# Operand addresses on multiples of 512 bytes, small tiles at the right edge, and centroid temporaries in the weight staging buffers

## The chip, the cores and the metric

The kernel runs on one core of a Trainium2 chip. The metric is the device time of one execution in microseconds; lower is better. A core has TensorE (PE; its weight loads are a row of their own, PEld), VectorE (DVE), ScalarE (ACT), GpSimd (POOL) and SyncE (SP), which here only issues DMAs. They work on SBUF, 128 partitions wide; an address below is a byte offset within a partition. PE writes to PSUM.

## The reference, cut to what matters

Three stages in float32. First an attention in which a key is seen by a query only if both are nearest to the same of 16 centroids of their head; then a mixer over tokens and channels; then a second one with a cosine and a sine.

```python
# attention, B=2, H=8, S=768, D=64, 16 centroids a head
q_assign = np.argmax(np.einsum('bhsd,hcd->bhsc', q_n, c_n), axis=-1)
k_assign = np.argmax(np.einsum('bhsd,hcd->bhsc', k_n, c_n), axis=-1)
mask = q_assign[:, :, :, None] == k_assign[:, :, None, :]
scores = np.where(mask, scale * np.matmul(q, k.transpose(0, 1, 3, 2)), -1000000000.0)
x = softmax(scores) @ v                       # then heads side by side: B x 768 x 512
# mixer 1
u = x + (np.maximum(xt @ w_tok1, 0.0) @ w_tok2).transpose(0, 2, 1)
x = u + np.maximum(u @ w_ch1, 0.0) @ w_ch2    # 512 -> 1536 -> 512
# mixer 2
theta = x @ w_theta
u = x + w_tok_r @ (x * np.cos(theta)) + w_tok_i @ (x * np.sin(theta))
out = u + np.maximum(u @ w_ch, 0.0)
```

The weights, q, k and v arrive as float32 or, for the weights, as float64 words.

## The kernel before, in words

**Products.** Each float32 operand is split into a high part (rounded to PE's one-pass float32 format, `F32R`) and a low part, the rest. A product then is three matmuls into one PSUM bank (`mm3`, L117 to L123): high by low, low by high, high by high. Every matmul has a stationary operand of 128 columns, which a weight load brings in, and a moving operand of 256, 384 or 512 columns that is streamed past it, four bytes a column and partition. Transposes (L408, L451, L562, L578, L702) are matmuls of 128 float32 columns against an identity matrix.

**Attention** (L156 to L510). Heads are taken in pairs. For a pair, `masks` (L240) multiplies queries and keys with the normalised centroids (tiles `csth`, `cstl`, stationary), transposes the similarities on DVE (tile `sT`), takes the maximum, compares, transposes back, keeps the first maximum with a triangular matrix (`pp`, L275) and leaves one-hot rows (`oh`, then `m`). They are appended to the query and key operands, so that `scores` (L381 to L388, out tile `s`, four matmuls of 384 columns) gives scores with the mask in them. A unit is two tiles of 128 queries of one head: `scores`, a row maximum on DVE (`nm`, L391), the exponential on ACT (`e`, L393), then `turn` (transposes `t` of `e`, and their split into `ph` and `pl`), then `values` (`o`, 12 matmuls of 256 columns). 48 units run in a software pipeline: unit n's scores, unit n-1's `turn`, unit n-2's `values`.

**The first pair.** Its masks need only the unsplit centroids `cst` (L250). `place_centroids` (L205 to L213) splits the centroids for the other pairs: a copy on ACT (`cth`), a subtraction on DVE (`ctl`), and then, after two memsets on POOL, four small casts on DVE that place them in `csth` and `cstl`. In the text it stands behind the first masks and the first heads' preparation (L469); the tile framework's scheduler, which orders each engine's instructions by its own simulation of the program, decides where they go.

**Mixers** (L524 to L734). Token mixing (`g`, `h`), then for channel mixing `r` (up, L617) and `c` (down, L625), then `th`, `y` and `po`, all with 512 columns (the last `po` in two halves). Each weight tile is loaded raw by DMA (512 KB into one of three buffers, tag `wraw`), converted on ACT, DVE and POOL, and split (`load_w`, L95).

**Where operands lie.** Tiles are carved out of pools one after the other, so small tiles shift what comes behind them. The program's allocation before, as the offset of each family of tiles modulo 512 bytes:

| tiles | role in products | offset mod 512 |
|---|---|---|
| `q2`, `k2`, `qh`, `k1` (`s`; q and k splits for `sim`) | both operands | 160 |
| `vs` | stationary of `o` | 160 |
| `e`, `ph`, `pl` | `ph`, `pl` moving of `o`; in token mixing moving of `g`, `h` | 416 |
| `uh/ul`, `rh/rl`, `zh/zl` (tag `blk`) | moving of `r` and `y`; stationary of `c`, `th` | 160 |
| weights' `h/l` parts (tag `wg`) | moving of `c`, `th`, `po`; stationary of `r`, `y` | 480 |
| `csth`, `cstl` | stationary of `sim` | 0 |
| `ident`, `xn` | transposes | 128 |

A slice of an operand starts a multiple of 512 bytes behind its tile's start, so these hold for slices too. The families at 480 lie in the upper part of SBUF (from byte 163808), those at 160 and 416 below byte 152000.

```python
halfpi = const.tile([P, 1], F32, name="halfpi")                       # L68
scratch = ap.tile([P, S], F32, tag="xt", bufs=2, name="scratch")      # L165
csth, cstl = (mp.tile([P, H // 2, 224], F32R, name=f"cst{k}") for k in "hl")  # L197
ct = ap.tile([P, NH], F32R, tag="m", bufs=2, name="ct")               # L198
sT = mp.tile([P, NH], F32, tag="sc", bufs=1, name=f"sT{b}{pr}")       # L255
```

Of the kernel before, what the change touches and what calls it, by code (L numbers as in the profile page):

```python
# [9 lines left out]
F32 = mybir.dt.float32  # L10
F32R = mybir.dt.float32r
# [7 lines left out]
P = 128  # L19
# [28 lines left out]
def tile_model(ctx: ExitStack, tc: tile.TileContext, qT, kT, v, cent, w1, w2, wc1, wc2, wth, wri, wch, out):  # L48
# [3 lines left out]
    B, H, D, S = qT.shape  # L52
    NT = S // P
    NH = S // 2
# [4 lines left out]
    NTT = w2.shape[1]  # L59
    scale = 1.0 / math.sqrt(D)  # L60

    const = ctx.enter_context(tc.tile_pool(name="const", bufs=1))

    marks = {}
    ident = const.tile([P, P], F32, name="ident")
    make_identity(nc, ident)
    xn = [const.tile([P, DM], F32, name=f"xn{i}") for i in range(B * NT)]
    halfpi = const.tile([P, 1], F32, name="halfpi")  # L68
    nc.gpsimd.memset(halfpi, math.pi / 2)


# [15 lines left out]
    wpool = ctx.enter_context(tc.tile_pool(name="wpool", bufs=1, side="right"))  # L87
# [68 lines left out]
    with ExitStack() as actx:  # L156
        ap = actx.enter_context(tc.tile_pool(name="attn", bufs=1))
# [4 lines left out]
        mp = mctx.enter_context(tc.tile_pool(name="mask", bufs=1, side="right"))  # L162


        scratch = ap.tile([P, S], F32, tag="xt", bufs=2, name="scratch")  # L165
        warm = scratch[:, 544:672].bitcast(BF16)
        nc.vector.memset(warm, 0.0)
        wps = ps_o.tile([P, 512], F32, tag="o", name="wps")
# [6 lines left out]
        c2 = scratch[:, 0 : 2 * D].rearrange("p (a d) -> p a d", a=2)  # L175
        nc.sync.dma_start(out=c2, in_=cent.unsqueeze(1).to_broadcast([P, 2, D]))
        csq = scratch[:, 2 * D : 3 * D]
        tiny = mp.tile([P, 1], F32, name="tiny")
        nc.vector.memset(tiny, 1e-30)
        cs = mp.tile([P, 6], F32, name="cs")  # L180
        nc.vector.tensor_tensor(out=csq, in0=c2[:, 0, :], in1=c2[:, 0, :], op=ALU.mult)
# [12 lines left out]


        cst = scratch[:, 192:416]
        csth, cstl = (mp.tile([P, H // 2, 224], F32R, name=f"cst{k}") for k in "hl")  # L197
        ct = ap.tile([P, NH], F32R, tag="m", bufs=2, name="ct")  # L198
        cth, ctl = ct[:, :P], ct[:, P : 2 * P]
        nc.gpsimd.memset(cst, 0.0)  # L200
        for j in range(2):
            r, n = slice(64 * j, 64 * j + 64), slice(96 + CL * j, 96 + CL * j + CL)
# [23 lines left out]
        )  # L226
        ltri = ltri.rearrange("p a c -> p (a c)")

        mab = mp.tile([P, 2], F32, name="mab")
        nc.gpsimd.memset(mab[0:64, 0:1], 1.0)  # L230
        nc.gpsimd.memset(mab[0:64, 1:2], 0.0)
        nc.gpsimd.memset(mab[64:128, 0:1], BIG)
# [7 lines left out]
        def masks(b, pr):  # L240


            ps = ps_t.tile([P, 512], F32, tag="t", name=f"sim{b}{pr}")[:, :NH]
            first = (b, pr) == (0, 0)
            src = raws if first else pairs[b, pr]
            for i in range(4):
                n = slice(i % 2 * NH, i % 2 * NH + NH)
                w = slice(96 - 32 * i, 224 - 32 * i)
                if first:
                    marks["sim"] = nc.tensor.matmul(ps, cst[:, w], src[i // 2][:, n], start=i == 0, stop=i == 3)  # L250
                else:
                    x = tuple(t[:, n] for t in src[i // 2 * 2 : i // 2 * 2 + 2])
                    mm3(ps, [((csth[:, pr, w], cstl[:, pr, w]), x)], i == 0, i == 3)

            sT = mp.tile([P, NH], F32, tag="sc", bufs=1, name=f"sT{b}{pr}")  # L255
            nc.vector.transpose(out=sT, in_=ps)
            yield
            s3 = sT.rearrange("p (n c) -> p n c", c=CL)
            mx = mp.tile([P, NH // CL], F32, tag="mx", bufs=2, name=f"mx{b}{pr}")
            nc.vector.tensor_reduce(out=mx, in_=s3, axis=AX.X, op=ALU.max)  # L260
            yield
            eq = mp.tile([P, NH], BF16, tag="eq", bufs=2, name=f"eq{b}{pr}")
            nc.vector.tensor_tensor(
                out=eq.rearrange("p (n c) -> p n c", c=CL), in0=s3,
                in1=mx.unsqueeze(2).to_broadcast([P, NH // CL, CL]), op=ALU.is_equal,
            )
            yield
            eqT = mp.tile([P, NH], BF16, tag="eq", bufs=2, name=f"eqT{b}{pr}")
            turned = nc.vector.transpose(out=eqT, in_=eq)
            marks.setdefault("eqT", turned)  # L270
            yield

            oh = mp.tile([P, NH], F32, tag="sc", bufs=1, name=f"oh{b}{pr}")
            pp = ps_t.tile([P, 512], F32, tag="t", name=f"pp{b}{pr}")[:, :NH]
            nc.tensor.matmul(pp, ltri, eqT, start=True, stop=True)  # L275
            nc.vector.scalar_tensor_tensor(out=oh, in0=pp, scalar=0.0, in1=eqT, op0=ALU.is_equal, op1=ALU.mult)
            if first:
                for a in range(2):
                    n = slice(a * NH, a * NH + NH)
                    r = 32 * a  # L280
                    nc.vector.tensor_copy(out=q2[0][64 : 64 + CL, n], in_=oh[r : r + CL, :])
                    r = 64 + 32 * a
                    if a == 0:
                        nc.scalar.activation(
                            out=k2[0][64 : 64 + CL, n], in_=oh[r : r + CL, :], func=AF.Copy, scale=BIG, bias=-BIG
                        )
                    else:
                        nc.vector.tensor_scalar(
                            out=k2[0][64 : 64 + CL, n], in0=oh[r : r + CL, :], scalar1=BIG, scalar2=-BIG,
                            op0=ALU.mult, op1=ALU.add,  # L290
                        )
            yield
            m = ap.tile([P, NH], F32R, tag="m", bufs=2, name=f"m{b}{pr}")
            nc.vector.tensor_scalar(
                out=m, in0=oh, scalar1=mab[:, 0:1], scalar2=mab[:, 1:2], op0=ALU.mult, op1=ALU.add
            )
            ms[b, pr] = m
# [49 lines left out]
        placed = [None]  # L347
# [25 lines left out]
        sums = {}  # L373
        xts = {}

        def scores(b, h, u, ops):

            qh, ql, k1, kk, _ = ops
            es = []
            for j in range(2):  # L380
                qt = 2 * u + j  # L381
                c = slice(qt * P, qt * P + P)
                ps = ps_s.tile([P, 2, 512], F32, tag="s", name=f"s{b}{h}{qt}")
                for half in range(2):
                    n = slice(half * NH, half * NH + NH)
                    nc.tensor.matmul(ps[:, half, :NH], qh[:, c], k1[:, n], start=True, stop=False)  # L386
                    last = nc.tensor.matmul(ps[:, half, :NH], ql[:, c], kk[:, n], start=False, stop=True)  # L387
                    if (b, h, u) == (0, 0, 0):  # L388
                        marks["scores"] = last
                nm = ap.tile([P, 1], F32, tag="nm", bufs=4, name=f"nm{b}{h}{qt}")  # L390
                nc.vector.tensor_reduce(out=nm, in_=ps[:, :, :NH], axis=AX.XY, op=ALU.max, negate=True)  # L391
                e = ap.tile([P, S], F32, tag="e", bufs=4, name=f"e{b}{h}{qt}")
                marks["exp"] = nc.scalar.activation(  # L393
                    out=e.rearrange("p (a n) -> p a n", a=2), in_=ps[:, :, :NH], func=AF.Exp,
                    bias=nm, accum_out=sums[b, h // 2][:, qt, h % 2 : h % 2 + 1],
                )
                es.append(e)
            return es
# [43 lines left out]
        def natural(b, pr):  # L442

            sm, xt = sums[b, pr], xts[b, pr]
            ri = ap.tile([P, NT, 2], F32, tag="ri", bufs=2, name=f"ri{b}{pr}")
            nc.vector.tensor_scalar(out=ri, in0=sm, scalar1=1e-9, scalar2=None, op0=ALU.add)
            nc.vector.reciprocal(out=ri, in_=ri)
            for q0, n in ((0, 4), (4, 2)):
                ps = ps_t.tile([P, 4, P], F32, tag="t", name=f"x{b}{pr}{q0}")
                for i in range(n):  # L450
                    nc.tensor.transpose(ps[:, i, :], xt[:, (q0 + i) * P : (q0 + i + 1) * P], ident)  # L451
                for i in range(n):
                    nc.vector.tensor_tensor(
                        out=xn[b * NT + q0 + i][:, pr * P : pr * P + P].rearrange("p (h d) -> p h d", h=2),
                        in0=ps[:, i, :].rearrange("p (h d) -> p h d", h=2),
                        in1=ri[:, q0 + i, :].unsqueeze(2).to_broadcast([P, 2, D]),
                        op=ALU.mult,
                    )
# [4 lines left out]
        for _ in masks(0, 0):  # L463
            pass
# [9 lines left out]
        for n in range(len(units) + SKEW):  # L474
            if n < len(units):
                b, h, u = units[n]
                if u == 0 and h % 2 == 0:
                    sums[b, h // 2] = ap.tile([P, NT, 2], F32, tag="sm", bufs=2, name=f"sm{b}{h}")
                    xts[b, h // 2] = ap.tile([P, S], F32, tag="xt", bufs=2, name=f"xt{b}{h}")
                es[n] = scores(b, h, u, ops[b, h])  # L480
                if n == 0:
# [8 lines left out]
                if p1 < len(heads) // 2:  # L490
                    pr = heads[2 * p1][0], heads[2 * p1][1] // 2
# [12 lines left out]
            if 0 <= n - SKEW:  # L504
                b, h, u = units[n - SKEW]
# [3 lines left out]
            while late and (n >= late[0][0] or n == len(units) + SKEW - 1):  # L509
                _, b, pr = late.pop(0)  # L510
# [212 lines left out]
    for n in range(len(steps) + 2):  # L723
        if n < len(steps):
            t, b = steps[n]
# [53 lines left out]
```

## Time and profile before

| | |
|---|---|
| time, median of 3 runs (lowest to highest) | 693.33 us (691.51 to 694.68) |
| the profiled execution's own time | 696.89 us |
| its span, first to last instruction | 694.7 us |
| mean granted TensorE clock | 0.983 |
| PE, busy share of the span | 96%, 3628 matmuls |
| DVE, ACT, POOL | 63%, 53%, 54% |

A matmul's duration in the profile holds its passage through the array, so matmuls that follow each other overlap, and "busy" says little of how fast they follow. What one costs in a dense stretch is the distance from its start to the start of the next; the timeline of PE shows it.

### The profile page before, as it was taken

What the parts mean: (1) busy time and instruction counts of PE and PEld (TensorE: products, weight loads), DVE (VectorE), ACT (ScalarE), POOL (GpSimd) and SP (SyncE); (2) the same over time, 40 slices, a digit from 0 to 9 for tenths busy, and PEclk for the clock granted to TensorE, in tenths of its full rate; (3) what the DMA queues carried; (4) which work ended last, traced back from release to release, by engine and by line L of the source; (5) the groups of instructions that cost most, each with busy time, mean ns of one, the idle gap of its engine ahead of it and who ended that gap; (6) DMA issues with size and microseconds to landing.
All of it is one profiled execution on the core that took longest, in us unless ns stands there. A gap on an engine that the chain in (4) does not pass through costs nothing.

```text
span 694.7 us, 10207 instructions
## 1 busy us (share of the span) xinstructions
PE 667.4 (96%) x3628; PEld 571.2 (82%) x3628; DVE 439.2 (63%) x704; ACT 368.1 (53%) x701; POOL 374.0 (54%) x359
## 2 busy tenths in 40 slices
PE   7799999999999997989999999999999999999998
PEld 4699999999999986868888888888887878888886
DVE  5698888988989988685544433444758776422112
ACT  3287878878788977465511530236668683320000
POOL 8558568589685873676622630421456787532000
PEclk8699999999999999989999999999999999999999
DMA  8447355474444412333410420120021323310001
GB/s 271 147 88 186 90 140 121 116 184 93 92 101 94 113 37 91 113 131 110 132 62 1 141 71 31 35 87 1 1 62 60 99 84 113 104 57 31 16 30 46
DMA packets 24530, 62.23 MB, mean 90 GB/s; under 512 B 4320, under 2 KB 7584, under 8 KB 24480
## 3 DMA queue, kind: packets, MB, share of 16 engines
q1 hardware_dynamic: 24480, 61.59, 31.8%
q8 instruction: 29, 0.48, 0.3%
q14 instruction: 21, 0.17, 0.1%
HBM read 40.44 MB, written 3.15 MB: 63 GB/s over the span
## 4 chain that ended last, share of the span: by engine, by line
PE 77%; DVE 6%; ACT 6%; POOL 4%; issue 3%; DMA 3%; SPq 1%; ACTq 0%; POOLq 0%; DVEq 0%
PE o L431 7%; PE t L408 6%; PE r L121 5%; PE r L123 5%; PE r L122 5%; PE c L123 5%; PE c L122 5%; PE c L121 5%; PE y L122 4%; PE y L123 4%; PE y L121 4%; PE s L386 4%; PE s L387 3%; ACT e L393 2%; PE po L121 2%
## 5 line engine op out<-in xcount | busy, mean ns | idle before, releaser
L393 ACT ACTIVATE e<-s,nm 128x768 f32<-128x768 f32 x96 | 86.8, 904 | 32.7 <-DVE nm L391 22.2
L391 DVE TENSOR_REDUCE nm<-s 128x1 f32<-128x768 f32 x96 | 90.8, 947 | 19.8 <-PE s L387 19.3
L386 PE MATMUL s<-k,qh 128*128 128x384 f32 x192 | 72.0, 376 | 8.3 <-ACT e L393 6.2
L408 PE MATMUL t<-ident,e 128*128 128x128 f32 x576 | 79.1, 275 | 0.8 <-DVE pl L85 0.5
L431 PE MATMUL o<-ph,vs 128*128 128x256 f32 x288 | 74.6, 293 | 3.9 <-DVE xt L438 3.9
L431 PE MATMUL o<-pl,vs 128*128 128x256 f32 x288 | 72.3, 285 | 0.0
L408 PEld LDWEIGHTS t<-ident,e 128*128 128x128 f32 x576 | 67.6, 142 | 5.6 <-PE s L387 1.1
L387 PE MATMUL s<-k,q 128*128 128x384 f32 x192 | 67.1, 350 | 1.6 <-ACT ct L84 1.6
L85 DVE TENSOR_TENSOR pl<-t,ph 128x512 fp32r<-128x512 f32 x96 | 63.4, 680 | 7.7 <-ACT ph L84 6.9
L419 POOL TENSOR_TENSOR pl<-pr,ph 128x512 fp32r<-128x512 f32 x48 | 62.8, 1308 | 1.8
L84 ACT ACTIVATE ph<-t 128x512 fp32r<-128x512 f32 x96 | 54.6, 597 | 16.8 <-PE t L408 11.9
L418 POOL TENSOR_SCALAR ph<-pr 128x512 fp32r<-128x512 f32 x48 | 30.9, 644 | 60.1 <-ACT pr L414 56.7
L431 PEld LDWEIGHTS o<-ph,vs 128*128 128x128 f32 x288 | 54.6, 190 | 5.9 <-DVE xt L438 5.7
L121 PE MATMUL r<-ul,c_h 128*128 128x512 f32 x144 | 58.5, 408 | 0.9 <-DVE ul L85 0.9
L122 PE MATMUL r<-uh,c_l 128*128 128x512 f32 x144 | 57.9, 402 | 0.0
L123 PE MATMUL r<-uh,c_h 128*128 128x512 f32 x144 | 57.6, 403 | 0.0
L121 PE MATMUL y<-zl,k_h 128*128 128x512 f32 x144 | 56.9, 395 | 0.0
L122 PE MATMUL y<-zh,k_l 128*128 128x512 f32 x144 | 56.8, 395 | 0.0
L123 PE MATMUL y<-zh,k_h 128*128 128x512 f32 x144 | 56.8, 395 | 0.0
L123 PE MATMUL c<-c_h,rh 128*128 128x512 f32 x144 | 56.6, 394 | 0.0
L122 PE MATMUL c<-c_h,rl 128*128 128x512 f32 x144 | 56.3, 392 | 0.0
L121 PE MATMUL c<-c_l,rh 128*128 128x512 f32 x144 | 55.3, 391 | 0.0
(204 smaller groups left out, 1622.0 us busy)
## 6 DMA issues: line engine op xcount, KB each, us to landing
c_raw<-wc SPq DMA_DIRECT2D x24, 512.0 KB, 3.4
k_raw<-wri SPq DMA_DIRECT2D x18, 512.0 KB, 3.6
qh<-qh SPq DMA_DIRECT2D x28, 192.0 KB, 3.0
k<-kh SPq DMA_DIRECT2D x28, 192.0 KB, 4.0
ql<-qT SPq DMA_DIRECT2D x8, 384.0 KB, 3.1
kl<-kT SPq DMA_DIRECT2D x8, 384.0 KB, 3.7
vr<-v SPq DMA_DIRECT2D x16, 192.0 KB, 2.6
w_raw<-w SPq DMA_DIRECT2D x6, 512.0 KB, 5.3
```

The source lines that it names most:

```text
L84: a = nc.scalar.activation(out=h, in_=ps, func=AF.Copy)
L85: return a, nc.vector.tensor_tensor(out=l, in0=ps, in1=h.bitcast(F32), op=ALU.subtract)
L121: nc.tensor.matmul(ps, ah, bl, start=first and i == 0, stop=False)
L122: nc.tensor.matmul(ps, al, bh, start=False, stop=False)
L123: nc.tensor.matmul(ps, ah, bh, start=False, stop=last and i == n - 1)
L386: nc.tensor.matmul(ps[:, half, :NH], qh[:, c], k1[:, n], start=True, stop=False)
L387: last = nc.tensor.matmul(ps[:, half, :NH], ql[:, c], kk[:, n], start=False, stop=True)
L391: nc.vector.tensor_reduce(out=nm, in_=ps[:, :, :NH], axis=AX.XY, op=ALU.max, negate=True)
L393: marks["exp"] = nc.scalar.activation(out=e.rearrange("p (a n) -> p a n", a=2), in_=ps[:, :, :NH], func=AF.Exp, bias=nm, accum_out=sums[b, ...
L408: nc.tensor.transpose(ps[:, a, i * P : i * P + P], es[i][:, kt * P : kt * P + P], ident)
L419: nc.gpsimd.tensor_tensor(out=pl, in0=raw, in1=ph.bitcast(F32), op=ALU.subtract)
L431: nc.tensor.matmul(ps[:, :256], vs[:, kt, :], p[:, kt % 2, :], start=n == 0 and k == 0, stop=n == NT - 1 and k == 1,)
```

## The change

- An empty tile of 96 float32 (`pad`) is put behind the constants, and all tiles of a few bytes (`halfpi`, `tiny`, `mab`, `nm`, `ri`, `sm`) go to a pool `small` at the right edge of SBUF. By the program's allocation after the change every family of the table stands at offset 0 modulo 512, `ident` and `xn` alone stay at 128.
- `scratch` and the placed centroids take the three buffers of the raw weights (tag `wraw`) instead of tiles in the attention's pools; `cth` and `ctl` are the last 128 columns of the tiles of `csth` and `cstl`.
- `sT` and `oh` have two buffers instead of one.

```diff
     const = ctx.enter_context(tc.tile_pool(name="const", bufs=1))
+    small = ctx.enter_context(tc.tile_pool(name="small", bufs=1, side="right"))
...
-    halfpi = const.tile([P, 1], F32, name="halfpi")
+    const.tile([P, 96], F32, name="pad")
+    halfpi = small.tile([P, 1], F32, name="halfpi")
...
-        scratch = ap.tile([P, S], F32, tag="xt", bufs=2, name="scratch")
+        scratch = wpool.tile([P, 1024], F32, tag="wraw", bufs=3, name="scratch")
...
-        csth, cstl = (mp.tile([P, H // 2, 224], F32R, name=f"cst{k}") for k in "hl")
-        ct = ap.tile([P, NH], F32R, tag="m", bufs=2, name="ct")
-        cth, ctl = ct[:, :P], ct[:, P : 2 * P]
+        placed = [wpool.tile([P, 1024], F32R, tag="wraw", bufs=3, name=f"cst{k}") for k in "hl"]
+        csth, cstl = (t[:, :896].rearrange("p (g n) -> p g n", n=224) for t in placed)
+        cth, ctl = (t[:, 896:] for t in placed)
...
-            sT = mp.tile([P, NH], F32, tag="sc", bufs=1, name=f"sT{b}{pr}")
+            sT = mp.tile([P, NH], F32, tag="sc", bufs=2, name=f"sT{b}{pr}")
...
-            oh = mp.tile([P, NH], F32, tag="sc", bufs=1, name=f"oh{b}{pr}")
+            oh = mp.tile([P, NH], F32, tag="sc", bufs=2, name=f"oh{b}{pr}")
...
-                nm = ap.tile([P, 1], F32, tag="nm", bufs=4, name=f"nm{b}{h}{qt}")
+                nm = small.tile([P, 1], F32, tag="nm", bufs=4, name=f"nm{b}{h}{qt}")
```

The other edits (`tiny`, `mab`, `ri`, `sm`) are of the last kind. The number and kind of instructions on every engine stay, and PE's order stays. What moves are the centroids' instructions on DVE, ACT and POOL at the start, and the first weights' DMAs on SP.

DVE at the start of the program, before the change: from the first pair's `eqT` to the first row maxima (`q`, `k` and `m` are the first heads' operands and masks).

```order
L269 STREAM_TRANSPOSE eqT_170<-eq_168 128x384
L311 SCALAR_TENSOR_TENSOR q_1_148<-qr_200,qh_206 64x768
L276 SCALAR_TENSOR_TENSOR oh_172<-pp_173,eqT_170 128x384
L281 CAST q_0_147<-oh_172 16x384 x2
L288 TENSOR_SCALAR k_0_149<-oh_172 16x384
L294 TENSOR_SCALAR m_180<-oh_172,mab 128x384
L85 TENSOR_TENSOR ct<-cps,ct 128x128
L211 CAST csth<-ct 64x4x16 x2
L211 CAST cstl<-ct 64x4x16 x2
L391 TENSOR_REDUCE nm_237<-s_232 128x1
L391 TENSOR_REDUCE nm_246<-s_241 128x1
```

The same engine after the change, from the copies of the unsplit centroids to the first pair's `eqT` (line numbers are three higher there).

```order
L206 COPY scratch<-cps 64x16 x2
L88 TENSOR_TENSOR cstl<-cps,csth 128x128
L214 CAST csth<-csth 64x4x16 x2
L314 SCALAR_TENSOR_TENSOR q_0_150<-qr_185,qh_191 64x768
L214 CAST cstl<-cstl 64x4x16 x2
L259 STREAM_TRANSPOSE sT_167<-sim_162 128x384
L263 TENSOR_REDUCE mx_169<-sT_167 128x24
L266 TENSOR_TENSOR eq_171<-sT_167,mx_169 128x384
L272 STREAM_TRANSPOSE eqT_173<-eq_171 128x384
```

The subtraction and the four casts have moved from between `m` and the first `nm` to ahead of the first pair's `sT`.

SP, which issues the DMAs, before the change, behind the first heads' loads (`w_0_raw` to `w_2_raw` are the first mixer's `w_tok1`, which is converted from 225.4 us on).

```order
L332 DMA kl_294<-kT 128x768
L332 DMA ql_685<-qT 128x768
L98 DMA w_0_raw<-w 128x1024
L332 DMA kl_687<-kT 128x768
L98 DMA w_1_raw<-w 128x1024
L322 DMA vr_535<-v 128x384
L98 DMA w_2_raw<-w 128x1024
L354 DMA q_1_148<-m_180 16x384 x2
L354 DMA k_1_150<-m_180 16x384 x2
```

And after it.

```order
L335 DMA kl_297<-kT 128x768
L335 DMA ql_688<-qT 128x768
L335 DMA kl_690<-kT 128x768
L325 DMA vr_538<-v 128x384
L357 DMA q_1_151<-m_183 16x384 x2
L357 DMA k_1_153<-m_183 16x384 x2
L325 DMA vr_683<-v 128x384
L101 DMA w_0_raw<-w 128x1024
```

`w_0_raw` is now issued behind the first masks; `w_1_raw` and `w_2_raw`, whose buffers hold the centroids, stand behind the key copies of the last pair's first head, some 120 rows further down.

## Rows read from the trace of the kernel before

**Rows 1.** Windows: busy us (and instructions) of PE, PEld, DVE, ACT, POOL; PEclk, DMA.

```profile
24.00:33.90 9.90, 7.54 (x24) 6.94 (x25) 4.22 (x5) 4.01 (x9) 2.88 (x3) 0.50 0.27 81
130.00:240.00 110.00, 108.56 (x807) 103.59 (x805) 97.55 (x168) 90.13 (x189) 82.25 (x86) 1.00 0.46 106
309.00:313.00 4.00, 4.00 (x11) 3.17 (x10) 3.55 (x7) 3.64 (x7) 2.81 (x3) 0.50 0.59 207
315.00:468.00 153.00, 153.00 (x668) 124.64 (x667) 65.24 (x99) 48.65 (x82) 60.76 (x52) 1.00 0.24 76
```

**Rows 2.** PE's groups by line and form: busy us, mean ns | idle before, releaser.

```profile
L431 PE MATMUL o<-ph,vs 128*128 128x256 f32 x288 | 74.6, 293 | 3.9 <-DVE xt L438 3.9
...
L386 PE MATMUL s<-k,qh 128*128 128x384 f32 x192 | 72.0, 376 | 8.3 <-ACT e L393 6.2 <-POOL k L314 2.0
...
L121 PE MATMUL r<-ul,c_h 128*128 128x512 f32 x144 | 58.5, 408 | 0.9 <-DVE ul L85 0.9
...
L121 PE MATMUL y<-zl,k_h 128*128 128x512 f32 x144 | 56.9, 395 | 0.0
...
L121 PE MATMUL c<-c_l,rh 128*128 128x512 f32 x144 | 55.3, 391 | 0.0
L121 PE MATMUL th<-th_l,x2h 128*128 128x512 f32 x48 | 19.0, 396 | 1.3 <-ACT x2h L84 1.3
...
L121 PE MATMUL po<-ch_l,u3h 128*128 128x512 f32 x44 | 18.3, 415 | 1.2 <-ACT u3h L84 1.2
```

**Rows 3.** PE's timeline (start us, us), `y`, moving operand at 160: first and nineteenth.

```profile
551.35 0.39 PE L121 MATMUL y<-zl,k_h 128*128 128x512 f32 x1
...
555.55 0.40 PE L121 MATMUL y<-zl,k_h 128*128 128x512 f32 x1
```

**Rows 4.** PE's timeline, `c`, moving operand at 480: first and twenty-eighth.

```profile
345.89 0.39 PE L121 MATMUL c<-c_l,rh 128*128 128x512 f32 x1
...
352.07 0.39 PE L121 MATMUL c<-c_l,rh 128*128 128x512 f32 x1
```

**Rows 5.** PE's timeline, `r` at half the clock: first and eleventh.

```profile
308.91 0.63 PE L122 MATMUL r<-uh,c_l 128*128 128x512 f32 x1
...
313.17 0.63 PE L123 MATMUL r<-uh,c_h 128*128 128x512 f32 x1
```

**Rows 6.** PE's timeline: 20 bf16 warm-up matmuls merged; eleven `o`; four `s`.

```profile
8.85 2.35 PE L171 MATMUL wps<-scratch 128*128 128x256 bf16 x20
...
150.86 0.28 PE L431 MATMUL o<-pl,vs 128*128 128x256 f32 x1
...
152.17 0.34 PE L386 MATMUL s<-k,qh 128*128 128x384 f32 x1
...
152.70 0.34 PE L387 MATMUL s<-k,q 128*128 128x384 f32 x1
```

**Rows 7.** DVE's timeline at the start.

```profile
8.77 0.95 DVE L311 SCALAR_TENSOR_TENSOR q<-qr,qh 64x768 fp32r<-64x768 f32 x1 [3.10 <-ACT qh L308]
...
11.55 0.58 DVE L269 STREAM_TRANSPOSE eqT<-eq 128x384 bf16<-128x384 bf16 x1
...
17.36 1.87 DVE L294 TENSOR_SCALAR m<-oh,mab 128x384 fp32r<-128x384 f32 x1
...
19.36 1.58 DVE L211 CAST csth<-ct 64x64 fp32r<-64x64 f32 x2
20.96 2.53 DVE L211 CAST cstl<-ct 64x64 fp32r<-64x64 f32 x2
23.53 1.82 DVE L391 TENSOR_REDUCE nm<-s 128x1 f32<-128x768 f32 x2
```

**Rows 8.** PE's timeline at the start.

```profile
13.23 0.86 PE L386 MATMUL s<-k,qh 128*128 128x384 f32 x2 [2.04 <-POOL k L314]
...
18.20 3.15 PE L171 MATMUL wps<-scratch 128*128 128x256 bf16 x18
25.56 0.69 PE L386 MATMUL s<-k,qh 128*128 128x384 f32 x1 [4.22 <-ACT e L393]
```

More of the change, by code (lines that the diff above doesn't have):

```diff
@@ L177, in tile_model @@
         csq = scratch[:, 2 * D : 3 * D]
-        tiny = mp.tile([P, 1], F32, name="tiny")
+        tiny = small.tile([P, 1], F32, name="tiny")
         nc.vector.memset(tiny, 1e-30)
@@ L227, in tile_model @@
         ltri = ltri.rearrange("p a c -> p (a c)")
-        mab = mp.tile([P, 2], F32, name="mab")
+        mab = small.tile([P, 2], F32, name="mab")
         nc.gpsimd.memset(mab[0:64, 0:1], 1.0)
@@ L444, in natural @@
             sm, xt = sums[b, pr], xts[b, pr]
-            ri = ap.tile([P, NT, 2], F32, tag="ri", bufs=2, name=f"ri{b}{pr}")
+            ri = small.tile([P, NT, 2], F32, tag="ri", bufs=2, name=f"ri{b}{pr}")
             nc.vector.tensor_scalar(out=ri, in0=sm, scalar1=1e-9, scalar2=None, op0=ALU.add)
@@ L477, in tile_model @@
                 if u == 0 and h % 2 == 0:
-                    sums[b, h // 2] = ap.tile([P, NT, 2], F32, tag="sm", bufs=2, name=f"sm{b}{h}")
+                    sums[b, h // 2] = small.tile([P, NT, 2], F32, tag="sm", bufs=2, name=f"sm{b}{h}")
                     xts[b, h // 2] = ap.tile([P, S], F32, tag="xt", bufs=2, name=f"xt{b}{h}")
```

## The prediction

> **What bounds the kernel now.** I read the windows first, then PE's groups, then PE's timeline in dense stretches, and last the timeline of the start. PE is covered almost without a gap: in the channel mixing 153.00 of 153.00 us, and in the attention 108.56 of 110.00, where DVE (97.55) and ACT (90.13) are not far behind [rows 1]. The groups name few waits of PE: 8.3 us before `s`, 3.9 before `o`, about 1 each before `r`, `th` and `po` [rows 2]. So what counts is how fast one matmul follows another, and that is read from starts.
>
> The reader is to see four distances. The 18 steps from 551.35 to 555.55 us give 233.3 ns for a matmul of 512 columns whose moving operand lies at 160 [rows 3]. The 27 steps from 345.89 to 352.07 give 228.9 ns where the moving operand lies at 480, 32 bytes short of a multiple of 512 [rows 4]. At a granted clock of 0.50, that is 1.2 GHz [rows 1], the same `r` takes 10 steps from 308.91 to 313.17, 426 ns, which halved is 213 [rows 5]: at the full clock 16 to 20 ns of each matmul are lost to something that half the speed doesn't show. And a stream of half as many bytes a column shows next to nothing of it: 20 bf16 matmuls of 256 columns in 2.35 us are 109 ns each once the last one's own 0.28 us are taken off, against 119.1 ns for `o` (11 steps from 150.86 to 152.17) [rows 6]. The four-byte moving stream at the full clock is thus limited by its reading, and where the operand starts seems to matter. `s`, 384 columns, takes 3 steps in 0.53 us, 176.7 ns [rows 6].
>
> **The change part by part.**
>
> *Alignment, the mixers.* At 160 lie the moving operands of `r` and `y` (three groups of 144 each), together 864 matmuls; at 480 those of `c`, `th` and `po`, 3 x (144 + 48 + 44) = 708 [rows 2]. `g` and `h` are few and left uncounted. No row has a four-byte moving operand at 0. The gain is bounded below by none, and above by the half-clock rate: 233.3 - 213 = 20 ns for the 864 and 228.9 - 213 = 16 ns for the 708, 17.3 + 11.3 = 28.6 us. I take the nearest row: an operand at 480 meets its first multiple of 512 after 8 columns, and one that starts on the multiple should be as good. So the 864 go to 228.9, 4.4 ns each, **3.8 us**, and the 708 keep their time. The reading behind it: each multiple of 512 met within the operand costs a little; 160 + 2048 bytes cross four, an aligned operand three; (233.3 - 213) / 4 is 5 ns, near the 4.4 seen.
>
> *Alignment, the attention.* I take the same share, 4.4 of 233.3 or 1.9%: 3.3 ns for 384 matmuls of `s` (two groups of 192) and 2.2 ns for 576 of `o` (two of 288), 1.3 + 1.3 us. Here DVE is 89% busy [rows 1], and PE does wait for ACT and DVE [rows 2], so I count three quarters, **1.9 us**. Bounds: none, and at the half-clock rate (160 and 107 ns) 6.4 + 7.0 = 13.4 us, of which again three quarters.
>
> *The start.* Before, `m` ends at 19.23 and the first row maximum starts at 23.53 [rows 7], though PE was through with its scores before the warm-up matmuls at 18.20 [rows 8]. Between them DVE subtracts and casts the centroids, 1.58 + 2.53 us for the casts alone [rows 7]. PE has run out of warm-up matmuls at 21.35 and waits for ACT's `e`, which waits for that maximum, until 25.56 [rows 8]. With the five instructions moved ahead of `sT`, the maximum follows `m`, 4.3 us sooner. What they cost in their new place: DVE idles 3.10 us before `q` at 8.77, which takes the subtraction and two casts; the other two come after `q` and put off `sT` and so `eqT`, which ended at 12.13, by up to 2.5 us [rows 7]. The next user of `eqT` is the matmul `pp`, and that stands on PE behind an `s` that POOL released only at 13.23 [rows 8], so 1.1 us of it is covered, and at worst 1.4 us of the 4.3 go back. The casts were slow while POOL worked beside them; I take 4.3 and keep 2.9 as the low end. PE's next scores then start at 21.4, right behind the warm-up. If the clock, at 0.50 from 24 to 33.9 us, stays up for it, the 24 matmuls that PE starts there [rows 1] gain up to 143 ns each (320 at half, 176.7 at full, for 384 columns), 3.4 us more; I don't count them. **4.3 us.**
>
> *The rest.* The three loads of `w_tok1` leave the start; two are issued behind the last pair's similarities, some 15 us ahead of the first conversion, so I cost them at nothing: DMA is busy 46% there [rows 1], and that spare time hides them. If it doesn't, the conversions come late and PE waits ahead of `g`. Behind those loads on SP stand the last head's values, not needed for two units. A second buffer for `sT` and `oh` frees DVE of waits on its own earlier work: nothing. Transposes keep their operands at 128: nothing.
>
> Sum: 3.8 + 1.9 + 4.3 = 10.0 us. The profiled execution took 696.9 us, 3.6 more than the median; taken off the median, 693.3 - 10.0 = **683.3 us**.
>
> **The rivals.**
>
> *An aligned stream loses nothing at all* (the cost is of requests that straddle a multiple, and aligned ones never do). For: 384 columns lose 17 of 160 ns and straddle three multiples, 256 lose 12 of 107 and straddle two, 512 lose 20 of 213 and straddle four, so the loss goes with that number as well. Against: at 480 as many are straddled, and the loss is a quarter less. The floor lies between 213 [rows 5] and twice 109 [rows 6]; with 216 for 512 columns: 864 x 17.3 + 708 x 12.9 = 24.1 us, and 7.4% of the attention's 384 x 176.7 + 576 x 119.1 ns, 10.1 us, three quarters of it 7.6. With the start 36.0: 657.3 us. The Trainium skill, "TensorE: Matmul & The Clock Gate", section "Back-to-back issue gap", gives N / 2.4 + 2.5 ns for any N, for 512 columns an estimate of 215.8, and names no address: by that rule nothing would be lost even now. The bf16 matmuls agree with it at 109 ns, the four-byte ones at 233.3 don't.
>
> *The offset means nothing; 480 was faster since those operands lie in the upper part of SBUF.* In the trace every moving operand at 480 lies high and every one at 160 low, so the rows can't tell. Then only the start gains: 689.0 us. The Trainium skill, "SBUF — State Buffer", section "Operand start alignment", asks only that an operand start at a multiple of its element's size, and says that its runs timed nothing; it has no 512.
>
> *Slower: all operands in one phase.* Now the moving stream and the weight load of the next matmul start at the same offset; if both then come upon the same place of the memory at once, every product loses. Against: `s` already has both operands at 160 and loses no larger share than `y`. Priced with the only step by offset that is seen: 1572 x 4.4 ns = 6.9 us and 1.9 in the attention, less the start's 4.3: slower by 4.5, 697.8 us. It decides from about 1.9 ns a product.
>
> **How the numbers follow.** Forecast 0.48, full rate 0.24, start only 0.17, one phase 0.07; 0.04 for the start's gain failing too, near 692. What a measurement of this kernel can tell from no change is about 0.5%, 3.5 us: below 689.8 or above 696.8. Forecast, full rate and two parts in three of the start-only case are faster: 0.82; same 0.11; slower 0.07. The range reaches from 653 (full rate, and the clock held at the start) to 690.5 (start only, with 1.4 us given back); the forecast's own is 679 to 686.
>
> **What would show it.** Right: `y` and `r` at about 229 ns from start to start, `c` unchanged; the first `nm` near 19.3 us; PE's second scores near 21.4. Full rate: all 512-column matmuls near 216. Start only: `y` still at 233. One phase: `c` above 229. The forecast is wrong if `y` and `c` don't meet, or if PE in the attention waits for DVE or ACT by as much as its matmuls gained.

## The result, and the profile after

| | before | changed |
|---|---|---|
| median (lowest to highest) | 692.69 us (691.51 to 694.68), 4 runs | 682.19 us (680.74 to 683.45), 4 runs |
| profiled execution, its span | 696.89, 694.7 us | 680.74, 679.0 us |
| mean granted clock of it | 0.983 | 0.997 |

The changed kernel is faster: ratio 0.9845, 95% interval 0.9809 to 0.9881, 10.5 us by the medians. Forecast was 683.3. The two profiled executions lie 16.1 us apart, since the one of before was 4.2 us above its median and the changed one 1.4 below; that surplus has to be found in the traces too, or a step of the change gets credit for it.

First the windows of the changed kernel, in the stretches of [rows 1] (busy us and instructions of PE, PEld, DVE, ACT, POOL; PEclk, DMA):

```profile
24.00:33.90 9.90, 9.90 (x70) 9.44 (x71) 7.57 (x12) 6.76 (x15) 5.83 (x6) 1.00 0.75 200
130.00:240.00 110.00, 108.53 (x806) 103.55 (x805) 97.25 (x170) 90.05 (x189) 87.56 (x91) 1.00 0.49 119
309.00:313.00 4.00, 4.00 (x19) 3.33 (x18) 1.41 (x3) 2.15 (x5) 3.50 (x3) 1.00 0.64 212
315.00:468.00 153.00, 153.00 (x684) 126.64 (x683) 65.62 (x100) 49.73 (x85) 56.94 (x48) 1.00 0.22 69
```

In the channel mixing PE is as full as before, 153.00 of 153.00 us, and puts 684 matmuls into it instead of 668. In the attention nothing moved: 806 for 807. And two stretches that ran at a clock of 0.50 now run at 1.00, so in 24 to 33.9 us PE starts 70 matmuls, not 24.

Next PE's timeline (start us, us) of the changed kernel: `y` and `c` with the nineteenth row behind the first, `s` and `o` in one dense stretch:

```profile
537.33 0.39 PE L126 MATMUL y<-zh,k_h 128*128 128x512 f32 x1
...
541.41 0.39 PE L126 MATMUL y<-zh,k_h 128*128 128x512 f32 x1
```

```profile
333.71 0.39 PE L124 MATMUL c<-c_l,rh 128*128 128x512 f32 x1
...
337.79 0.39 PE L124 MATMUL c<-c_l,rh 128*128 128x512 f32 x1
```

```profile
148.67 0.34 PE L390 MATMUL s<-k,q 128*128 128x384 f32 x1
...
149.19 0.28 PE L434 MATMUL o<-ph,vs 128*128 128x256 f32 x1
...
150.50 0.28 PE L434 MATMUL o<-pl,vs 128*128 128x256 f32 x1
```

`y` and `c` now both take 4.08 us for 18 steps, 226.7 ns; before they were 233.3 [rows 3] and 228.9 [rows 4]. `o` takes 1.31 us for 11 steps, 119.1 ns, what it took before [rows 6]. `s`, three steps in 0.52 us, is at 173; over all its steps under 190 ns the mean is 175.5 before and 175.4 after.

Last, how far ahead the changed kernel is. These are the lines of five tiles (count, ns of one at least, in the middle and at most, first and last start), of before and then of the change:

```profile
L451 PE MATMUL x<-ident,xt x48: 270/272/333, 69.6 to 273.6; 128*128 128x128 f32 x48
L121 PE MATMUL g<-xl,w_h x24: 388/394/506, 252.0 to 289.8; 128*128 128x512 f32 x24
L121 PE MATMUL r<-ul,c_h x144: 392/398/767, 308.3 to 521.8; 128*128 128x512 f32 x144
L121 PE MATMUL c<-c_l,rh x144: 387/389/478, 344.5 to 536.0; 128*128 128x512 f32 x144
L121 PE MATMUL y<-zl,k_h x144: 391/394/481, 548.1 to 681.4; 128*128 128x512 f32 x144
```

```profile
L454 PE MATMUL x<-ident,xt x48: 270/272/331, 62.3 to 266.5; 128*128 128x128 f32 x48
L124 PE MATMUL g<-xl,w_h x24: 389/389/499, 244.8 to 282.3; 128*128 128x512 f32 x24
L124 PE MATMUL r<-ul,c_h x144: 389/389/476, 300.9 to 508.3; 128*128 128x512 f32 x144
L124 PE MATMUL c<-c_l,rh x144: 389/389/476, 333.7 to 522.4; 128*128 128x512 f32 x144
L124 PE MATMUL y<-zl,k_h x144: 389/389/476, 534.4 to 665.3; 128*128 128x512 f32 x144
```

The lead is 7.3 us at the first `x`, 7.2 at the first `g`, 7.4 at the first `r`: all of it comes from the start, none from the attention. At the first `c` it is 10.8; most of that step is the half-clock stretch of before around 310 us [rows 1], which this execution lacks. From there to the last `y` it grows by 5.3 to 16.1: the mixers' matmuls.

The start itself, DVE and then PE of the changed kernel:

```profile
6.81 0.63 DVE L214 CAST csth<-csth 64x64 fp32r<-64x64 f32 x2
...
9.32 1.30 DVE L214 CAST cstl<-cstl 64x64 fp32r<-64x64 f32 x2
...
12.91 0.58 DVE L272 STREAM_TRANSPOSE eqT<-eq 128x384 bf16<-128x384 bf16 x1
...
16.95 1.87 DVE L297 TENSOR_SCALAR m<-oh,mab 128x384 fp32r<-128x384 f32 x1
18.74 1.81 DVE L394 TENSOR_REDUCE nm<-s 128x1 f32<-128x768 f32 x2
```

```profile
13.54 0.32 PE L278 MATMUL pp<-eqT,ltri 128*128 128x384 bf16 x1 [0.41 <-DVE eqT L272]
...
17.78 2.86 PE L174 MATMUL wps<-scratch 128*128 128x256 bf16 x18
20.76 0.46 PE L389 MATMUL s<-k,qh 128*128 128x384 f32 x1
```

The first row maximum follows `m` at 18.74, 4.8 us sooner than in [rows 7], and PE's second scores start at 20.76, right behind the warm-up matmuls, 4.8 sooner than in [rows 8]. Of these 4.8 us, 0.4 come from `m` itself, which begins at 16.95 and not at 17.36. `eqT` is 1.4 us later than before and `pp` waits 0.41 us for it.

### The profile page after: what moved, and what is told of

Read it like the earlier page. It is cut to its first block, busy times and chain, and to the rows that moved or that the text cites. A ratio compares the mean times of both kernels' runs of the same rounds, so it can differ in the third digit from the quotient of the medians.

```text
span 679.0 us, 10216 instructions
## 1 busy us (share of the span) xinstructions
PE 653.7 (96%) x3628; PEld 564.8 (83%) x3628; DVE 437.1 (64%) x704; ACT 367.2 (54%) x701; POOL 374.1 (55%) x359
## 4 chain that ended last, share of the span: by engine, by line
PE 77%; DVE 7%; ACT 6%; issue 3%; POOL 3%; DMA 3%; SPq 1%; ACTq 0%; POOLq 0%; DVEq 0%
PE o L434 7%; PE t L411 6%; PE r L124 5%; PE r L125 5%; PE r L126 5%; PE c L124 5%; PE c L125 5%; PE c L126 5%; PE y L126 4%; PE y L124 4%; PE y L125 4%; PE s L389 4%; PE s L390 3%; ACT e L396 2%; PE po L124 2%
## 5 line engine op out<-in xcount | busy, mean ns | idle before, releaser
L124 PE MATMUL r<-ul,c_h 128*128 128x512 f32 x144 | 56.6, 394 | 1.1 <-DVE ul L88 1.1
L125 PE MATMUL r<-uh,c_l 128*128 128x512 f32 x144 | 56.1, 389 | 0.0
L126 PE MATMUL r<-uh,c_h 128*128 128x512 f32 x144 | 55.8, 390 | 0.0
```

Of the source, the lines that this page charges most:

```text
L124: nc.tensor.matmul(ps, ah, bl, start=first and i == 0, stop=False)
L125: nc.tensor.matmul(ps, al, bh, start=False, stop=False)
L126: nc.tensor.matmul(ps, ah, bh, start=False, stop=last and i == n - 1)
```

## The experiments

**What about the offsets?** Three kernels put the fillers so that the operands' families lie at 160 or 0 on the left of SBUF and at 480 or 0 on the right; everything else is the changed kernel, the start too.

```diff
-    const.tile([P, 96], F32, name="pad")
+    const.tile([P, 136], F32, name="pad")       # left at 160: all_off, left_off
+    small.tile([P, 8], F32, name="edge")        # right at 480: all_off, right_off
```

Both families off, the left at 160 and the right at 480:

> The changed kernel with its two empty tiles sized so that every family stands as before the change: 160 modulo 512 on the left, 480 for the weights' parts on the right (ph and pl at 160 instead of 416). The order at the start is the changed one. If offset makes the mixers' gain: the lead at the start stays at 7.6 us, y and r go back to 233.3 ns a matmul and c to 229, the time is about 6 us above the changed kernel, 688 us. If the mixers' gain comes from something else in the change (the buffers, the order), y stays at 227 and the time at 682.

Measured: 688.40 us (10 runs; ratio to before 0.9945, 0.9919 to 0.9971), with `r` and `y` at 233 again and `c` at 230.9 on the mean, not 229. So the offsets are worth 6.2 us by the medians (6.9 by the ratios, give or take 3), and the new start, with the loads and buffers that moved along, the remaining 4.5. Then one side at a time:

> Only the left families at 160 (moving of r and y, stationary of c and th; all of the attention), the weights' parts at 0. If the moving operand's offset decides: y and r 233, c and th 227. If the stationary operand's decides: y and r 227, c and th 229 or more. If both add: y 233 or less, c between. s and o as in the changed kernel (175 and 119 ns) either way, since the alignment did not change them.

> Only the weights' parts at 480 (stationary of r and y, moving of c, th and po), the left families at 0. Moving decides: y and r 227, c 229. Stationary decides: y and r 233, c 227.

Measured, one execution each: 691.58 and 691.75 us. Neither the moving nor the stationary operand decides by itself: with either side off, `y` and `r` are at 233 to 234. `c`, too, is slowed to 233, as PE's timeline shows for the kernel with the left at 160 and the right at 0 (18 steps in 4.20 us):

```profile
342.83 0.39 PE L125 MATMUL c<-c_h,rl 128*128 128x512 f32 x1
...
347.03 0.39 PE L125 MATMUL c<-c_h,rl 128*128 128x512 f32 x1
```

Its moving operand lies on a multiple of 512 there, and it is slower than the 229 of the kernel before, where it lay at 480. What all fast cases share is that both operands start at the same place modulo 512. That was my new theory, and the next run was made to break it: nothing on a multiple, but both families at 160.

```diff
-    const.tile([P, 96], F32, name="pad")
+    const.tile([P, 136], F32, name="pad")
+    small.tile([P, 88], F32, name="edge")
```

> The changed kernel with both families of operands moved from 0 to 160 modulo 512, so no operand of a product lies at a multiple any more, but the two operands of each product still start at the same offset. If what counts is that the two operands of a product share their offset: every 512-column group at 227 ns, as at 0, and the time of the changed kernel, about 682. If what counts is the multiple of 512 itself: 233 ns everywhere, and about 688, as with the operands at 160 and 480.

Measured: 683.52 us, ratio 0.9847 (0.9813 to 0.9881), the changed kernel's. PE's timeline, `y`, 18 steps in 4.08 us again:

```profile
540.39 0.39 PE L127 MATMUL y<-zh,k_h 128*128 128x512 f32 x1
...
544.47 0.39 PE L127 MATMUL y<-zh,k_h 128*128 128x512 f32 x1
```

So the multiple of 512 is not what helps. To see which differences count, streams of 24 independent products on zeros were put ahead of the changed kernel, 26 of them and then 25 more:

```diff
+        for name, cols, mo, so, mcols in [("first", 512, 0, 0, 128)] * 4 + MB:
+            ps = bps.tile([P, 512], F32, tag="mb", name=f"mb{name}")
+            for i in range(24):
+                x = mo // 4 + i % 2 * 512
+                w = so // 4 + i % 4 * 256
+                nc.tensor.matmul(ps[:mcols, :cols], sta[:, w : w + mcols], mov[:, x : x + cols], start=True, stop=True)
```

> The changed kernel with 26 streams of 24 four-byte products ahead of it, on zeros, each with its own pair of offsets modulo 512 of moving and stationary operand, with 512, 384 and 256 columns, and four of them with only 32 columns of weights in place of 128. A shared offset decides: the streams at (0,0), (160,160) and (256,256) at 227 ns, all other pairs at 229 to 234. The multiple decides: only (0,0) at 227. The loss is the weight load's reading beside the moving stream: with 32 columns of weights 216 ns or less at both offsets. For 384 and 256 columns, where the change gained nothing although 256 went from unequal to equal offsets: 175 and 119 whatever the offsets, if the short ones are limited by something else. The streams add about 130 us to the time, which is of no interest.

PE's timeline of it; a row is one stream, and its time per product is the distance to the next row's start over 24:

```profile
26.61 5.61 PE L86 MATMUL mba<-mov,sta 128*128 128x512 f32 x24
32.06 5.64 PE L86 MATMUL mbb<-mov,sta 128*128 128x512 f32 x24
37.54 5.77 PE L86 MATMUL mbc<-mov,sta 128*128 128x512 f32 x24
43.15 5.77 PE L86 MATMUL mbd<-mov,sta 128*128 128x512 f32 x24
...
65.53 5.61 PE L86 MATMUL mbh<-mov,sta 128*128 128x512 f32 x24
70.98 5.75 PE L86 MATMUL mbi<-mov,sta 128*128 128x512 f32 x24
...
133.54 4.33 PE L86 MATMUL mbu<-mov,sta 128*128 128x384 f32 x24
137.70 4.32 PE L86 MATMUL mbv<-mov,sta 128*32 128x384 f32 x24
141.86 3.03 PE L86 MATMUL mbw<-mov,sta 128*128 128x256 f32 x24
144.73 3.03 PE L86 MATMUL mbx<-mov,sta 128*128 128x256 f32 x24
147.60 3.04 PE L86 MATMUL mby<-mov,sta 128*128 128x256 f32 x24
```

Stream `a` has both operands at 0, `b` both at 160, `c` moving 0 and stationary 160: 227.1, 228.3 and 233.7 ns. `h` has moving 0 and stationary 256, and takes 227.1: a difference of 256 bytes is as good as none. A second set, made the same way, fills in the steps:

> The changed kernel with another set of streams of 24 products ahead of it, on zeros. If the difference of the two starts counts modulo 256, as the first table says: 227 ns at differences of 0 and 256 and 232 to 234 at 64, 96, 128, 160, 192 and 224, for 384 columns 173 at a shared phase and 177 otherwise; small differences of 4 and 16 bytes are open (227 if a granule of 32 or 64 bytes is what counts, 233 if not). If it were the moving operand's own start, (64,64) would be slow. Two-byte operands (512 columns): 216 ns at any offsets, if the loss is one of the four-byte reads; 227 and more if it is of every product. The fixed 13.3 ns that four-byte products take above their columns at 2.4 GHz (512: 226.7, 384: 173.4, 256: 119.8): if it is the change of weights, it goes where the same weights are used by all 24 products; if it is the rows that are read, it halves with 64 partitions.

Time per product by the start of the moving minus the start of the stationary operand, modulo 256, from both sets, four-byte operands of 512 columns (two numbers, or a range: other pairs of offsets with the same difference):

| difference | 0 | 4 | 16 | 32 | 64 | 96 | 128 | 160 | 192 | 224 |
|---|---|---|---|---|---|---|---|---|---|---|
| ns | 226.7 to 228.3 | 237.1 | 231.7 | 232.5, 233.3 | 229.2, 230.0 | 233.7 | 232.1 to 233.3 | 233.7 | 232.9 to 233.7 | 232.9 to 233.7 |

The kernels fit into it. Before, `r` and `y` had 160 and 480, a difference of 192; `c` had 480 and 160, a difference of 64, the one that costs only some 2 ns; `s` 160 and 160, and `o` 416 and 160, a difference of 256: both were at the good phase already. With 384 columns the streams take 173.3 to 174.2 ns in phase, 173.3 at 64, 174.6 at 192 and 177.1 at 96; with 256 columns 119.6 at 0 and at 96, and 118.0 at 64.

The trace of the kernel before had a row that tells the two operands apart. [rows 3] and [rows 4] don't, and the table of families says that the moving operands of `g` lie at 416; but the first batch takes them from the tag `wg` (`tok_x` with `part`), so that moving and stationary operand both lie at 480. PE's timeline of the kernel before, second and twelfth of the first `g`:

```profile
252.35 0.39 PE L122 MATMUL g<-xh,w_l 128*128 128x512 f32 x1
...
254.61 0.39 PE L123 MATMUL g<-xh,w_h 128*128 128x512 f32 x1
```

These are 10 steps in 2.26 us, 226 to 227 ns each, with no operand on a multiple of 512. The second batch of the same `g`, against the same weights but with its moving operand at 416, takes 16 steps from 286.54 to 290.27 us, 233 ns.

Even in phase a four-byte product stays above its columns at 2.4 GHz by 13.4 ns at 512 (226.7 - 213.3), 13.3 at 384 (173.3 - 160), 12.9 at 256 (119.6 - 106.7): much the same price at three lengths. Two-byte operands don't pay it, in the second set, at differences of 0, 64 and 192 with 512 columns and then 0 and 192 with 256:

```profile
111.45 5.35 PE L102 MATMUL mbba<-mov,sta 128*128 128x512 bf16 x23
116.64 5.34 PE L102 MATMUL mbbb<-mov,sta 128*128 128x512 bf16 x24
121.82 5.34 PE L102 MATMUL mbbc<-mov,sta 128*128 128x512 bf16 x23
127.00 2.78 PE L102 MATMUL mbbd<-mov,sta 128*128 128x256 bf16 x24
129.62 2.78 PE L102 MATMUL mbbe<-mov,sta 128*128 128x256 bf16 x24
```

These are 216 and 109 ns at all of these offsets. The 13 ns of the four-byte products did not go with one set of weights for all 24 products, nor with 64 partitions (227 from start to start inside both streams), and not with 32 columns of weights (231 in phase at 512 columns, 173 at 384). So neither the change of weights nor the number of rows or weight columns explains them, and their cause stays open.

**A longer period?** The same kernel with every family of the mixers at a multiple of 2048 (`pad` of 352 elements, `edge` of 384):

> The changed kernel with every operand's family at a multiple of 2048 bytes and not only of 512 (a larger filler on the left, a filler of 1536 bytes on the right). If the place modulo 512 is all that counts: 227 ns and the changed kernel's time, about 682, no difference. If a longer period counts as well, so that the 11 ns that 227 is above the 216 of the clock have to do with it: towards 216 ns, up to 1572 x 11 ns = 17 us less, down to 665.

Measured: 682.69 us, 0.9845 (0.9814 to 0.9876), `y` and `c` at 227. A longer period, up to 2048 bytes, doesn't show.

**The start.** The order undone alone, with the offsets of the change kept:

```diff
-        place_centroids()
+        with tc.issue_after(marks["m"].ins):
+            place_centroids()
```

> The changed kernel, all aligned, with the centroids' subtraction and casts held on DVE until behind the first m, as before the change. If the order at the start makes the lead: the first row maximum starts near 23.5 us instead of 18.7, PE's second scores near 25.5 instead of 20.8, the clock falls to half from 24 us on, and the time rises by 7 to 7.6 us to about 689.5. If only the wait counts and the clock holds: by 4.5 us. If the lead has another source (the weights' loads that left the start): no change.

Measured: 686.45 us, ratio 0.9893 (0.9843 to 0.9943), with `r`, `c` and `y` at 227. DVE's timeline has the casts between `m` and the maximum again, which comes at 21.17 and not at 18.74:

```profile
16.65 0.87 DVE L297 TENSOR_SCALAR m<-oh,mab 128x384 fp32r<-128x384 f32 x1
...
17.63 1.81 DVE L214 CAST csth<-csth 64x64 fp32r<-64x64 f32 x2
19.47 1.67 DVE L214 CAST cstl<-cstl 64x64 fp32r<-64x64 f32 x2
21.17 1.82 DVE L395 TENSOR_REDUCE nm<-s 128x1 f32<-128x768 f32 x2
```

The maximum was expected near 23.5 us, where it was before. This run takes back 2.4 of the 4.8 us: `m` is done at 17.52 here, at 19.23 before [rows 7], and the casts take 3.5 us instead of 4.1. What sets `m` and the casts back in the kernel before was not taken apart. The second scores come at 23.21, the clock is at half from 23.1 to 26.5 us, and at the first `x` this trace is 2.8 us behind the changed kernel's.

By the medians the order is worth 4.3 us here; with the offsets off the whole new start is worth 4.5. By the ratios these are 3.3 and 3.8. The 3.8 is known to 1.8 us either way; the 3.3 is a difference of two ratios and by itself not clear of nothing, but the four times here (685.45 to 686.88) all lie above the four of the changed kernel (up to 683.45). The lead at the first `x` was 7.3, though. Part of the rest should be the clock of [rows 1], and that can be tried in the kernel before, by filling PE's idle stretch with more warm-up matmuls:

```diff
-WARM = (17, 4, 20, 18)
+WARM = (17, 4, 20, 44)
```

> The kernel before with 44 instead of 18 warm-up products behind the first scores, so that PE's idle stretch of 21.35 to 25.56 us is filled; order and alignment stay as before. If 3.3 of the start's 7.6 us are the clock alone, the granted clock stays at 1.0 behind 25.56 us and the kernel gains about 3 us: 689 to 690, with the second scores still at 25.6. If the start's gain is all the earlier row maximum, nothing: 692.7. If the warm-up runs at half speed it ends at 27.6 and delays the second scores by 2 us.

The windows of this kernel, the stretch that was at 0.50 in [rows 1]:

```profile
24.00:33.90 9.90, 8.56 (x57) 7.75 (x56) 6.91 (x9) 5.97 (x13) 3.13 (x3) 1.00 0.41 117
```

The second scores start at 25.79, as late as before, but 57 matmuls start in the stretch, not 24, and 48 us into the span the kernel is 3.3 us ahead of the profiled execution of before at the same matmul, 2.3 from 105 us on: that is the clock's share in that pair of traces. Yet the time is 691.88 us against 693.03, ratio 0.9992 (0.9964 to 1.0019): the median moved by 1.2 us, and the interval, -2.5 to +1.3 us, leaves no room for 3. The expectation of 689 to 690 failed there. The mean clock of the 13 executions of before beside it goes from 0.983 to 0.998, and what one trace loses to it is not what the median loses.

**What was costed at nothing.** One buffer for `sT` and `oh`, as before:

```diff
-            sT = mp.tile([P, NH], F32, tag="sc", bufs=2, name=f"sT{b}{pr}")
+            sT = mp.tile([P, NH], F32, tag="sc", bufs=1, name=f"sT{b}{pr}")
...
-            oh = mp.tile([P, NH], F32, tag="sc", bufs=2, name=f"oh{b}{pr}")
+            oh = mp.tile([P, NH], F32, tag="sc", bufs=1, name=f"oh{b}{pr}")
```

> The changed kernel with one buffer in place of two for the similarities' transposes and for the one-hot masks, as before. The prediction costs the second buffer at nothing: 682.2. If part of the 4.3 us of the start, or the attention's free stretches, hang on it: 683 to 687.

Measured: 683.94 us, 0.9859 (0.9812 to 0.9906). The interval holds the changed kernel's ratio; a microsecond either way would not be seen. Its profile lies 4.3 us behind the one of the change, over half of it lost in and behind a half-clock stretch from 300.8 to 307.6 us.

**A try at more.** Such a half-clock stretch comes up near 300 us in most of the traces, behind waits of PE for DVE in the turns `u` ahead of the channel mixing. The last of the three turns isn't needed by the first products `r`:

```diff
-    u_turn(2)
...
+                if (f0, f, ch) == (0, 0, 2):
+                    u_turn(2)
                 rs[f, ch] = up(f0 + f, ch, w)
```

> The changed kernel once more, as it is, beside the next one on the same chip: 682.2, ratio to the kernel before 0.9845. If the profiled execution is one with a half-clock window near 300 us, as in five of the experiments, it is some 3.4 us longer than the one shown of the changed kernel, at the same spacing of 227 ns.

> The changed kernel with the third of the three turns of the token-mixed activations moved behind the first two products r of the channel mixing, which don't need it. In the trace of the changed kernel PE waits there for DVE's ul four times between 296.5 and 300.9 us, 2.7 us together, and most executions have a half-clock window of 6.8 us right behind, which costs up to 3.4 us. If r can start on the first two turns: 2.7 us less, 679.5, and without the window up to 3.4 more, 676 at the best. If ACT and DVE, which turn the u and convert the weights, are the limit there anyway, PE waits as long a little later: no change, 682.2.

Measured side by side: the change again 683.60 us (0.9856, 0.9827 to 0.9885), the variant 685.65 (0.9893, 0.9865 to 0.9921), no gain and 2 us behind by the medians. The profiled execution of the change again is 3.3 us longer than the one shown above, at the same 227 ns; its half-clock stretch, 303.0 to 306.4 us, can account for 1.7 of them. PE's timeline of the variant tells why it gains nothing:

```profile
309.20 0.52 PE L124 MATMUL r<-ul,c_h 128*128 128x512 f32 x1 [3.19 <-DVE ul L88]
```

The third alternative came nearest, that PE waits as long a little later: the four short waits, 2.7 us together, became two of 0.63 and 0.68 us and this one, since DVE makes the `ul` of the third turn as much later, and the half clock follows the wait (from 309.5 to 313.0 us). It said no change, though, and the variant is 2 us slower.

## Why the prediction was right, and where only its sum was

*The start, 4.3 us.* Right in mechanism, and in size within what was measured: the maximum follows `m`, the second scores follow the warm-up, `pp` waits for `eqT` by 0.4 us instead of the 1.4 allowed for. The maximum comes 4.8 us sooner for the 4.3 forecast, and the whole new start is worth 4.5 us by the medians. That the order of the casts alone makes all of it is not shown: undoing it put the maximum back by 2.4 us. The 3.4 us of clock that were named and not counted are real in the profiled pair, 2.3 to 3.3 by the experiment, but not shown in the medians; leaving them out of a forecast of the median came out better.

*Alignment, the mixers, 3.8 us.* Right in sign, wrong in mechanism, too small. The step that failed is "an operand at 480 meets its first multiple of 512 after 8 columns, and one that starts on the multiple should be as good". The offsets of the two operands were read one at a time, from rows in which they always changed together: 160 with 480, and 480 with 160. It is their difference modulo 256 that counts, as the kernel with everything at 160 shows, and the table. `g` of the kernel before, left uncounted, would have told, and so would the count of multiples: at 480 four are crossed as at 160, which the prediction holds against its first rival and not against its own reading. So `r` and `y` went past 228.9 to 227, and `c`, which was to stay, gained as well. By the means of all steps at the full clock in the two traces, `r` went from 233.3 to 227.5, `y` from 233.2 to 226.8, `c` from 229.0 to 227.0, `th` from 229.7 to 227.3, and `po` from 229.8 to 230.9. Behind the first `c`, 288 `r` x 5.8, 432 `y` x 6.4, 432 `c` x 2.0 and 144 `th` x 2.4 ns, less 132 `po` x 1.1, are 5.5 us, of which the lead shows 5.3; with the 144 `r` ahead of it 6.3, and by the medians of the runs without the offsets it is 6.2.

*Alignment, the attention, 1.9 us.* Wrong: nothing, neither in the spacing of `s` and `o` nor in the lead. The same step: a share of `y`'s loss was carried over to operands that were in phase already. The reading behind it, about 5 ns for each multiple crossed, fitted 512, 384 and 256 columns alike by accident; what those lose in phase is about 13 ns a product, whatever it crosses. That this loss is one of reading the moving stream, as the prediction has it, no run shows.

*The rest, nothing.* Nothing was found: the attention's windows are alike, and the second buffer gives no measurable difference. The loads of `w_tok1` were not tried alone; `g` is neither earlier nor later against `x` (7.3, then 7.2 us of lead).

*The rivals.* Full rate would have needed 216 ns; the best of the four-byte streams is 227. The Trainium skill, "TensorE: Matmul & The Clock Gate", section "Back-to-back issue gap", gives N / 2.4 + 2.5 ns as the gap of an isolated matmul, by estimate 215.8 ns for 512 columns and 109.2 for 256, beside some 131 ns measured in a stream of 512 columns: the two-byte streams here agree with the formula (216 and 109), the four-byte ones stand at N / 2.4 + 13 in phase, and none shows 131. "The offset means nothing" is refuted by 6.2 us between two kernels that differ in their fillers only. The slower rival had the right pair of quantities and the wrong sign: one phase is what makes the products fast. The argument against it, that `s` "loses no larger share than `y`", doesn't hold by the prediction's own numbers, 17 of 160 ns against 20 of 213; and at its price of 8.8 us for 4.4 ns it would have eaten up the start's 4.3 us from 2.1 ns a product, not 1.9.

So 3.8 + 1.9 + 4.3 = 10.0 met 10.5 by luck: 2.4 us too little in the mixers stood against 1.9 too much in the attention. The time was right, and two of its three terms were not.

## What to carry to other kernels

When a stream of four-byte matmuls of 512 columns is spaced wider than 227 ns at the full clock, compare the starts of its moving and its stationary operand modulo 256 bytes and move one of the two families by a filler: equal starts are enough, a multiple of anything is not needed, and at most differences tried it is worth 6 to 7 ns a product in a long run of them, up to 4 at 384 columns and nothing seen at 256. Before pricing an offset, check whether the rows let you tell one operand's offset from the other's; those chosen here didn't, a group left out as too small did, and so did a short table of streams. And when two profiled executions differ by more than their medians, take the half-clock stretches out before crediting the change.

## What the runs showed of the hardware that was not expected

The speed of a four-byte product of 512 columns depends on the distance of its two operands modulo 256 bytes: 227 to 228 ns at 0, 229 to 230 at 64, 232 to 234 at 16, 32 and the others tried, 237 at 4. It isn't symmetric: 64 costs 2.5 ns, 192 costs 6.6.

At a difference of 64 a stream has two paces. In the trace of the kernel before all long runs of `c` go at 229.0 ns; in that of the kernel with 44 warm-up matmuls, which has the same offsets, and in that of the kernel with both families off, the first run of 144 goes at 233.3 from end to end and the second at 229.0. Which one a run takes up, and why, stays open; so `c` gains 2 ns in the pair shown and 3.9 on the mean against these two.

In phase a stream doesn't start at 227 ns. Nine of the eleven groups of `po` begin behind four transposes; PE's timeline of the changed kernel, second and eleventh product of one of them:

```profile
575.67 0.40 PE L125 MATMUL po<-ch_h,u3l 128*128 128x512 f32 x1
...
577.76 0.39 PE L125 MATMUL po<-ch_h,u3l 128*128 128x512 f32 x1
```

The step before these was 314 ns; these nine last from 224 to 236 ns each, 232 on the mean, and only then come steps of 227. That is why `po` stays at 230.9 ns in the changed kernel, though its operands start alike.

Two-byte products of 512 columns take 216 ns at the three distances tried. And the 13 ns of a four-byte product are not there at half the clock: [rows 5] has 426 ns, and 512 columns at 1.2 GHz are 426.7. What they are, no run here settles.
